# K of head 0's second half as one transfer of 128 rows, c and x as four transfers of four rows

## The chip, the cores and the metric

The kernel runs on one core of one Trainium2 chip, one launch per call. The metric is the device time of a run in microseconds (us). All times below are of the kernel with the inputs of the reference, all in bf16.

## The reference

One token passes a conditioned transformer block: an attention over a cache of 32768 positions with 8 KV heads and 32 query heads, then a small ReLU network. Cut to what matters:

```python
mod = (silu(c) @ w_mod).reshape(1, 6, 1, 512)         # c: (1, 512), w_mod: (512, 3072)
sa, ca, ga, sb, cb, gb = mod[:, 0], ..., mod[:, 5]
h = layernorm(x) * (1 + ca) + sa                      # x: (1, 1, 512)
q = (h @ wq) in 32 heads of 128                       # wq: (512, 4096)
o = softmax(q k^T / sqrt(128)) v, per head            # k, v: (8, 32768, 128), 4 query heads to each
x = x + ga * (o @ wo)                                 # wo: (4096, 512)
h = layernorm(x) * (1 + cb) + sb
x = x + gb * (relu(h @ w1) @ w2)                      # w1: (512, 1792), w2: (1792, 512)
```

K and V are 8.39 MB per head each, 134 MB together, and the weights are 15 MB. Each byte is read from HBM once and used once.

## The kernel before

The kernel is a stream of loads with the arithmetic hung beneath it. The list `stream` (lines 163 to 169) names the loads in order: K of head 0 in two halves with `w_mod` and `wq` between them, then for each head g the K of head g + 1 and the V of head g, the last heads in halves and quarters, then `wo`, `w1` and `w2` in pieces. `need(key)` (L172) issues loads from the list until the one that is asked for is out; `load` (L112) finds place and source of one; `stream_dma` (L154) issues it from SP (SyncE), so nearly all bytes go through SP's one queue. The name `UNEVEN` (L57) singles out one load, the second half of head 0's K: it goes out in three transfers (L137 to L142). The first has all 128 rows of this half without their last 512 bytes (32256 of 32768 bytes a row), the second has these last 512 bytes of rows 0 to 110, the third those of rows 111 to 127.

K and V tiles of one head (64 KB in each of 128 partitions) lie in a ring of three places. The first place holds `w_mod` and `wq`, the second K of head 0, the third K of head 1, then V of head 0 takes the first, and so on. So a load waits until the tile before it in its place has been used: V of head 0 for the last use of `wq`'s place (the product that spreads q, L409), K of head 2 for the scores of head 0 (L460). A transfer's completion is also told by one of eight semaphores in turn, and a transfer that reuses a semaphore waits for the one before on it.

`c` and `x` (512 values each) come in from ACT's queue (L182, L183) as two transfers of 8 rows of 64 values into `cx_row`. VectorE (DVE) spreads them (L248), TensorE (PE) turns them into columns (L254), and from there come silu(c) (L313 to L318) and the sums of the first layer norm (L279 to L307). Then PE multiplies silu(c) with `w_mod` (L324), the six parts of the modulation are turned back into columns (L339 to L346), the normalised h is finished (L307), q is formed with `wq` (L396) and spread (L403 to L411).

For each head, DVE transposes K in blocks of 32x32 (L332 for the first half of head 0, L441 for the rest), PE forms the scores (L460), DVE and ACT make the softmax of it (L473 to L509), and PE multiplies with V (L523). The order on PE and DVE is written out by hand (L637 to L795). In the end PE runs through `wo`, `w1` and `w2` as they land (L599, L765, L788), two DVE operations make the output (L793, L795) and SP stores it (L796).

Of the kernel before, what the change touches and what calls it, by code (L numbers as in the profile page):

```python
# [17 lines left out]
def kernel(  # L18
# [14 lines left out]
    nc = tc.nc  # L33
    P = 128
    _, _, D = A_x.shape
    _, Hkv, Sk, Dh = A_k_cache.shape
# [6 lines left out]
    TK = 64  # L43
# [10 lines left out]

    OUT0, OUT1 = 30, 34

    UNEVEN, EDGE, MOST = ("k", 0, (2, 3)), 2 * TK * Dh - D // 2, 111  # L57
    SPACE = 14
    assert Dh == 128 and REP == 4 and D == 512 and FT == W2P[-1][1] and NTILE == 4
    scale = float(Dh) ** -0.5  # L60
# [9 lines left out]
    def wo_v(i):  # L70
        g0, n = WOP[i]
        return A_wo[g0 * REP * Dh:(g0 + n) * REP * Dh, :].rearrange("(p r) d -> p r d", p=P)
# [33 lines left out]
    def piece(name, at, n):  # L106

        if name not in pieces:
            pieces[name] = ring.tile([P, NTILE * TK * Dh], BF16, tag="slot", name=name)
        return pieces[name][:, at:at + n]  # L110

    def load(key):  # L112
        kind = key[0]
        if kind == "wm":
            t = piece("wmq_sb", 0, WM).rearrange("p (kt n) -> p kt n", kt=KT)
            src = wm_v
        elif kind == "wq":
            t = piece("wmq_sb", WM, WQ).rearrange("p (kt n) -> p kt n", kt=KT)
            src = wq_v
        elif kind in "kv":  # L120
            g, steps = key[1], key[2]
            src = (kv if kind == "k" else vv)[g, :, TK * steps[0]:TK * (steps[-1] + 1), :]
            name = f"Ksb{g}" if kind == "k" else f"Vsb{g}"
            t = piece(name, TK * Dh * steps[0], TK * Dh * len(steps)).rearrange("p (j d) -> p j d", d=Dh)
        elif kind == "wo":
            g0, n = WOP[key[1]]
            t = piece("tail_sb", g0 * REP * D, n * REP * D).rearrange("p (r d) -> p r d", d=D)
            src = wo_v(key[1])
        elif kind == "w1":
            k0, k1 = W1P[key[1]]  # L130
            t = piece("tail_sb", WO + k0 * Dff, (k1 - k0) * Dff).rearrange("p (kt f) -> p kt f", f=Dff)
            src = w1_v[:, k0:k1]
        else:
            f0, f1 = W2P[key[1]]
            t = piece("tail_sb", WO + KT * Dff + f0 * D, (f1 - f0) * D).rearrange("p (f d) -> p f d", d=D)
            src = w2_v[:, f0:f1]
        if key == UNEVEN:  # L137
            row, src_row = (x.rearrange("p j d -> p (j d)") for x in (t, src))
            for rows, cols in (
                (slice(0, P), slice(0, EDGE)), (slice(0, MOST), slice(EDGE, None)), (slice(MOST, P), slice(EDGE, None)),  # L140
            ):
                stream_dma(row[rows, cols], src_row[rows, cols])  # L142
        else:
            stream_dma(t, src)
        if key[:2] == ("v", 0):
            for _ in range(SPACE):
                nc.sync.drain()
        if kind in "kv":
            for i, u in enumerate(steps):
                loaded[(kind, g, u)] = t[:, TK * i:TK * (i + 1), :]  # L150
        else:
            loaded[key] = t

    def stream_dma(dst, src):  # L154
        i = nc.sync.dma_start(out=dst, in_=src)  # L155
        tc.stamp_issue_order_token(i.ins, "sp_stream")
        if last_loop:

            tc.add_manual_dep(i.ins, last_loop[0], mybir.DependencyInfo(
                mybir.DependencyClass.NoSync, mybir.DependencyReason.DATA))  # L160
# [11 lines left out]
    def need(key):  # L172
        while key not in loaded:
            load(stream[pos[0]])
            pos[0] += 1
        return loaded[key]
# [3 lines left out]
    wm_sb = need(("wm",))  # L180
    cx_row = const.tile([16, D // 8], BF16)
    for i, row in enumerate((c[0], A_x[0, 0])):  # L182
        nc.scalar.dma_start(out=cx_row[8 * i:8 * i + 8], in_=row.rearrange("(a n) -> a n", a=8))  # L183

    ident_bf = const.tile([P, P], BF16)
    make_identity(nc, ident_bf[:])
# [10 lines left out]
        out=sel.rearrange("p (h par) (a c) -> p h par a c", h=2, a=4),  # L197
        in_=AP(ib.tensor, ib.offset, [ib.ap[0], [64, 2], [1, 2], [0, 4], [2, 32]]),
# [8 lines left out]
        out=mask16.rearrange("p (s q) -> p s q", q=REP),  # L207
        in_=AP(ident_f[:].tensor, ident_f[:].offset, [ident_f[:].ap[0], [0, 4], [1, REP], [REP, P // REP]]),
# [4 lines left out]
    for n in sorted({n * REP for _, n in WOP}):  # L213
        cmask[n] = const.tile([P, P // n], F32, name=f"cmask{n}")
        nc.vector.tensor_reduce(
            out=cmask[n][:], in_=ident_f[:].rearrange("p (c r) -> p c r", r=n), op=ALU.add, axis=AX.X,
# [3 lines left out]
            out=rsel_f[:], in_=ident_f[:].rearrange("p (c r) -> p r c", r=n), op=ALU.add, axis=AX.X,  # L220
# [6 lines left out]
        out=smask[:], in_=ident_f[0:16, 0:16].rearrange("p (s q) -> p s q", q=REP), op=ALU.add, axis=AX.X,  # L227
# [7 lines left out]
        out=place32[:], in_=ident_f[:].rearrange("p (j m) -> p m j", m=32), op=ALU.add, axis=AX.X,  # L235
# [4 lines left out]
        out=rowpick[:, OUT0:OUT1], in_=ident_f[:].rearrange("p (j m) -> p j m", m=32), op=ALU.add, axis=AX.X,  # L240
# [8 lines left out]
        out=cx_bd, in0=cx_row[:].unsqueeze(1).to_broadcast([16, 8, D // 8]),  # L249
# [80 lines left out]
    for u in range(2):  # L330
        t = need(("k", 0, u)).rearrange("p j d -> p (j d)").bitcast(F32)
# [30 lines left out]
    def four_rows(e, name):  # L362
# [16 lines left out]
        out=nca[:], in0=modT_sb[:, KT:2 * KT], scalar1=-1.0, scalar2=-1.0, op0=ALU.mult, op1=ALU.add,  # L379
# [3 lines left out]
        out=ncb[:], in0=modT_sb[:, 4 * KT:5 * KT], scalar1=-1.0, scalar2=-1.0, op0=ALU.mult, op1=ALU.add,  # L383
# [18 lines left out]
    for i in range(2):  # L402
        nc.vector.transpose(out=q_cols[:, i, :], in_=q_ps[i])  # L403
        nc.scalar.copy(
            out=qT_sb[:, 16 * i:16 * (i + 1)], in_=q_cols[:, i, :].rearrange("p (h r) -> p h r", r=32)[:, :, 0],
# [231 lines left out]
    with tc.manual_schedule(engines={mybir.EngineType.PE, mybir.EngineType.DVE}):  # L637
# [54 lines left out]
        for u in (2, 3):  # L692
# [49 lines left out]
            out=x1T[:], in0=x1T[:], scalar=1.0, in1=xT, op0=ALU.mult, op1=ALU.add, accum_out=stat2[:, 0:1],  # L742
# [31 lines left out]
        for f0, f1 in ((0, FT // 2), (FT // 2, FT)):  # L774
            nc.vector.transpose(out=hidT[:, f0:f1], in_=hid_v[:, f0:f1])
            nc.scalar.activation(
                out=AP(hb.tensor, hb.offset + 32 * f0 + 31, [hb.ap[0], [32, f1 - f0]]),
                in_=hidT[:, f0:f1, 0], func=ACT.Relu,
            )

        for part, (f0, f1) in enumerate(W2P):
            w2_sb = need(("w2", part))
            for ft in range(f0, f1):
                for i in (0, 2, 1, 3):
                    row = OUT0 + i
# [41 lines left out]
```

## Time and profile before

| what | value |
|---|---|
| time, median of 3 runs | 354.38 us (354.29 to 354.51) |
| the profiled execution | 354.42 us |
| its span, first to last instruction | 352.6 us |
| PE busy | 272.3 us, 77% of the span |
| DVE busy | 195.6 us, 55% |
| ACT busy | 18.7 us, 5% |
| transfers of SP's queue (q1), share of the 16 DMA engines | 98.5% |
| granted TensorE clock, mean | 0.926 |

How to read it: the busy shares are of one core's engines over the whole span; the share of a DMA queue is the time of all its packets over 16 engines times the span. A packet is one contiguous run of bytes, or the 4 bytes with which one DMA engine tells that its part of a transfer has landed. The rate in GB/s of a slice counts each packet where it starts, so in a slice of a few hundredths of a us a single row of K (32 or 64 KB) stands out as a large number. Times in the views count from the first instruction; between the span and the time of a run lie 354.42 - 352.6 = 1.8 us that no instruction fills.

### The profile page before, as it was taken

How to read it: one execution, taken by the hardware profiler on the slowest of the kernel's cores; microseconds unless marked ns; L12 is line 12 of the kernel's file. 1: busy time of each engine (PE TensorE's matmuls, PEld its weight loads, DVE VectorE, ACT ScalarE, POOL GpSimd, SP SyncE). 2: the span in 40 equal slices, each digit the busy share in tenths (PEclk: the TensorE clock that was granted, in tenths of full speed). 3: DMA queues.
4: the chain of work that ended last, by engine and by line, in shares of the span. 5: the costliest groups of instructions: out<-in, count | busy, mean ns of one | idle time of the engine just before them, and what ended most of it. 6: DMA issues, size and time to landing. Idle time of an engine off the chain costs nothing. (4 is left out here: it accounts for less than half of the span.)

```text
span 352.6 us, 3544 instructions
## 1 busy us (share of the span) xinstructions
PE 272.3 (77%) x1310; PEld 111.8 (32%) x1310; DVE 195.6 (55%) x167; ACT 18.7 (5%) x37; POOL 6.0 (2%) x26
## 2 busy tenths in 40 slices
PE   0054980695999679884988499976999999789994
PEld 0021330232333224331333233322444443234442
DVE  7662563983079513965099316956674293743142
ACT  1200003001000010001000100001000100011000
POOL 3000000000000000000000000000000000000000
PEclk9996895698999969998999979996999999999999
DMA  8999989999999999999999999999999999999995
GB/s 353 404 432 456 468 387 461 446 401 446 439 424 440 416 439 446 401 455 446 409 453 446 409 453 431 426 394 439 446 414 427 450 429 424 431 453 398 432 426 213
DMA packets 5222, 149.57 MB, mean 424 GB/s; under 512 B 604, under 2 KB 988, under 8 KB 1628
## 3 DMA queue, kind: packets, MB, share of 16 engines
q1 hardware_dynamic: 5180, 149.43, 98.5%
q8 instruction: 8, 0.13, 0.1%
q14 instruction: 2, 0.02, 0.0%
q10 hardware_dynamic: 32, 0.00, 0.0%
HBM read 149.42 MB, written 0.00 MB: 424 GB/s over the span
## 5 line engine op out<-in xcount | busy, mean ns | idle before, releaser
L441 DVE STREAM_TRANSPOSE Ksb<-Ksb 128x4096 f32<-128x4096 f32 (+1 forms) x34 | 131.5, 3912 | 57.6 <-DMA Ksb<-in_A_k_cache_dram 57.6
L460 PE MATMUL S_ps<-Ksb,qbd 128*128 128x512 bf16 x512 | 118.9, 385 | 19.2 <-DVE Ksb L441 18.3
L523 PE MATMUL o_ps<-Vsb,P_g 128*16 (+1 forms) x512 | 124.3, 401 | 10.9 <-ACT P_g L497 10.0
L460 PEld LDWEIGHTS <-qbd 128*128 128x128 bf16 x512 | 49.2, 97 | 84.9 <-issue 27.6
L523 PEld LDWEIGHTS o_ps<-Vsb,P_g 128*16 x320 | 30.4, 95 | 60.0 <-issue 31.8
L523 PEld LDWEIGHTS <-P_g 128*16 128x16 bf16 x192 | 16.7, 90 | 22.9 <-issue 0.4
L473 DVE TENSOR_REDUCE m_p<-S_ps 128x1 f32<-128x1024 f32 x7 | 8.6, 1223 | 21.8 <-PE S_ps L460 21.8
L502 DVE STREAM_TRANSPOSE P_g<-P_g 128x1024 bf16<-128x1024 bf16 x8 | 10.0, 1245 | 15.6 <-ACT P_g L497 15.6
L494 ACT ACTIVATE nbias<-Mb_ps 128x1 f32<-128x1 f32 x8 | 1.4, 171 | 269.5 <-PE Mb_ps L492 269.5
L324 PE MATMUL mod_ps<-wmq_sb,siluT 128*1 128x512 bf16 x24 | 3.6, 624 | 9.9 <-DMA wmq_sb<-in_w_mod_dram 9.9
L332 DVE STREAM_TRANSPOSE Ksb<-Ksb 128x4096 f32<-128x4096 f32 x2 | 8.8, 4424 | 1.7 <-DMA Ksb<-in_A_k_cache_dram 1.7
L478 PE MATMUL mT_ps<-ident_f,m_p 128*1 128x128 f32 x8 | 2.2, 270 | 8.9 <-DVE m_p L473 7.9
L497 ACT ACTIVATE P_g<-S_ps,nbias 128x1024 bf16<-128x1024 f32 x8 | 8.9, 1114 | 0.2
L560 PE MATMUL acc_ps<-mask_sb,Y 16*128 16x4 f32 x16 | 3.4, 282 | 5.1 <-DVE Y L556 5.1
L552 DVE SCALAR_TENSOR_TENSOR o_ps<-o_ps,Linv,smask 16x512 f32<-16x512 f32 x8 | 5.8, 720 | 2.8 <-PE o_ps L523 2.8
L254 PE MATMUL xc_ps<-cx_sel,wmq_sb 16*128 16x2 bf16 x4 | 0.3, 172 | 8.7 <-DVE wmq_sb L248 8.7
L590 DVE CAST o_sb<-o_ps 128x4 bf16<-128x4 f32 (+2 forms) x4 | 0.7, 167 | 11.1 <-PE o_ps L586 11.1
L415 POOL TENSOR_TENSOR qbd<-qrep_sb,rowpick 128x64 bf16<-128x64 bf16 x8 | 2.4, 299 | 228.0 <-PE S_ps L460 198.3
L509 DVE RECIPROCAL Linv<-L_ps 16x1 f32<-16x1 f32 x8 | 1.0, 126 | 8.3 <-PE L_ps L506 8.3
L556 DVE TENSOR_REDUCE Y<-o_ps 16x128 f32<-16x512 f32 x8 | 5.4, 679 | 0.3
L635 PE MATMUL spare_ps<-qbd,ident_bf 128*128 128x512 bf16 x18 | 5.4, 381 | 0.0
L396 PE MATMUL q_ps<-wmq_sb,hT 128*1 128x512 bf16 x32 | 3.6, 626 | 2.3 <-DMA wmq_sb<-in_A_wq_dram 2.3
(114 smaller groups left out, 71.6 us busy)
## 6 DMA issues: line engine op xcount, KB each, us to landing
Ksb<-in_A_k_cache_dram SPq DMA_DIRECT2D x5, 4096.0 KB, 22.9
Vsb<-in_A_v_cache_dram SPq DMA_DIRECT2D x5, 4096.0 KB, 36.5
wmq_sb<-in_A_wq_dram SPq DMA_DIRECT2D x1, 4096.0 KB, 28.1
Vsb<-in_A_v_cache_dram SPq DMA_DIRECT2D x2, 2048.0 KB, 41.1
Ksb<-in_A_k_cache_dram SPq DMA_DIRECT2D x1, 4032.0 KB, 37.2
wmq_sb<-in_w_mod_dram SPq DMA_DIRECT2D x1, 3072.0 KB, 18.9
tail_sb<-in_A_wo_dram SPq DMA_DIRECT2D x1, 2048.0 KB, 23.2
tail_sb<-in_B_w_dram SPq DMA_DIRECT2D x1, 1792.0 KB, 30.6
```

The lines of the kernel that those rows point to most:

```text
L324: nc.tensor.matmul(dst[j // 4][32 * (j % 4):32 * (j % 4) + 1, :], lhsT=src_T[:, kt:kt + 1], rhs=w[:, kt, j * 512:(j + 1) * 512], start=(kt ...
L332: nc.vector.transpose(out=t, in_=t)
L396: nc.tensor.matmul(q_ps[i][32 * a:32 * a + 1, :].rearrange("o (h e) -> o h e", e=32), lhsT=hT[:, kt:kt + 1], rhs=wq_f[:, kt, i, a], start= ...
L441: t = nc.vector.transpose(out=KTt.bitcast(F32), in_=KTt.bitcast(F32))
L460: nc.tensor.matmul(S_ps_tiles[g], lhsT=qbd[g % 2][:, hp, 4 * (7 - s):4 * (7 - s) + P], rhs=KTv[:, 16 * sl:16 * sl + 16, h, :, par], start= ...
L473: behind_loop(nc.vector.reduce_max(out=m_p[:], in_=S_g.rearrange("p g f -> p (g f)"), axis=AX.X))
L497: nc.scalar.activation(out=P_g[:], in_=S_g.rearrange("p g f -> p (g f)"), func=ACT.Exp, bias=nbias[:], scale=scale, accum_out=l_g[:],)
L502: behind_loop(nc.vector.transpose(out=P_g[:], in_=P_g[:]))
L523: nc.tensor.matmul(o_tiles[g][:], lhsT=PT, rhs=Vx, start=first, stop=False, skip_group_check=True)
L552: nc.vector.scalar_tensor_tensor(out=o, in0=o, scalar=Linv_tiles.pop(g)[:], in1=smask[:].unsqueeze(2).to_broadcast([16, 4, Dh]), op0=ALU.m ...
L556: nc.vector.tensor_reduce(out=Y[:], in_=o.rearrange("p s d -> p d s"), op=ALU.add, axis=AX.X)
L635: nc.tensor.matmul(spare[0], lhsT=ident_bf[:], rhs=qbd[0][:, :, 0:P], start=True, stop=True)
```

## The change

The name `UNEVEN` and its three transfers go: the second half of head 0's K is one transfer of 128 rows of 32768 bytes, as all other halves are. And `c` and `x` go out as four transfers of 4 rows in the place of two of 8 rows. The number of transfers stays the same, 3 + 2 before and 1 + 4 after, and so the later transfers keep their turn among the eight semaphores. The order of all other instructions on every engine is unchanged.

```diff
-    UNEVEN, EDGE, MOST = ("k", 0, (2, 3)), 2 * TK * Dh - D // 2, 111
     SPACE = 14
...
-        if key == UNEVEN:
-            row, src_row = (x.rearrange("p j d -> p (j d)") for x in (t, src))
-            for rows, cols in (
-                (slice(0, P), slice(0, EDGE)), (slice(0, MOST), slice(EDGE, None)), (slice(MOST, P), slice(EDGE, None)),
-            ):
-                stream_dma(row[rows, cols], src_row[rows, cols])
-        else:
-            stream_dma(t, src)
+        stream_dma(t, src)
...
     for i, row in enumerate((c[0], A_x[0, 0])):
-        nc.scalar.dma_start(out=cx_row[8 * i:8 * i + 8], in_=row.rearrange("(a n) -> a n", a=8))
+        for a in (0, 4):
+            nc.scalar.dma_start(
+                out=cx_row[8 * i + a:8 * i + a + 4], in_=row.rearrange("(a n) -> a n", a=8)[a:a + 4],
+            )
```

## The prediction

> **What bounds the kernel now.** I read the page's DMA part first, then the chain of work that ended last, then windows over the DMA traffic.
>
> ```profile
> span 352.6 us, 3544 instructions
> ...
> DMA packets 5222, 149.57 MB, mean 424 GB/s; under 512 B 604, under 2 KB 988, under 8 KB 1628
> ...
> q1 hardware_dynamic: 5180, 149.43, 98.5%
> q8 instruction: 8, 0.13, 0.1%
> ...
> q10 hardware_dynamic: 32, 0.00, 0.0%
> ```
>
> SP's queue keeps the 16 DMA engines busy for 98.5% of the span. The chain, in order of time, ends so:
>
> ```profile
> 338.50 11.12 DMA tail_sb<-in_B_w_dram
> ...
> 349.66 0.29 PE end_ps L788 x4
> ...
> 350.30 0.28 DVE o_bf L795
> ```
>
> The last piece of `w2` lands at 349.6 us and all that follows is under 3 us of fixed work. So the end is the end of the stream. Is the stream ever dry? The columns that count here are the last two, DMA share and GB/s:
>
> ```profile
> 12.85:21.62 8.77, 1.51 (x16) 0.51 (x17) 8.77 (x3) 0.00 (x0) 0.00 (x0) 1.00 1.01 433
> 60.00:77.00 17.00, 12.23 (x48) 5.07 (x49) 16.73 (x4) 0.00 (x0) 0.00 (x0) 0.76 1.00 432
> 200.00:300.00 100.00, 90.01 (x395) 37.65 (x396) 57.49 (x39) 4.13 (x9) 0.30 (x1) 0.93 1.00 430
> 347.80:349.60 1.80, 1.33 (x34) 1.01 (x32) 0.00 (x0) 0.00 (x0) 0.00 (x0) 1.00 0.44 158
> ```
>
> It isn't: 432 GB/s, 27.0 a DMA engine, throughout. But in the last 1.8 us the share is 0.44: some engines are done while others still carry data. The last transfer is complete when its slowest engine is, so the time is set by the engine with the most to do, and I have to ask which one that is.
>
> **The split, engine by engine.** This is the DMA traffic from 38.57 to 39.88 us in 40 slices of 33 ns, as the pieces of head 0's K go by and K of head 1 begins:
>
> ```profile
> GB/s 16 4065 2032 31 10069 31 63 4034 31 4081 47 94 2048 63 78 47 78 63 63 78 47 78 63 47 94 47 78 2048 31 47 47 47 31 47 47 47 2017 16 31 2001
> DMA packets 164, 1.11 MB, mean 851 GB/s; under 512 B 20, under 2 KB 148, under 8 KB 148
> ```
>
> A slice near 2000 is one 64 KB row of K of head 1, an engine's first (4065 is two, 10069 five). Thirteen engines reach it in slices 2 to 13, by 39.0 us. Three come in slices 28, 37 and 40, at 39.46, 39.76 and 39.86: these carry the 148 - 20 = 128 packets of 512 bytes. The one with the longest queue is 38 slices, 1.25 us, behind the first, the shortest 26 slices, 0.85. So 111 rows went to three engines at 37 each, and the 17 rows to one of the three (54 there): 0.85 / 37 is 23 ns a packet.
>
> Is one of these three the last at the end? The same view from 58.15 to 59.95 us (45 ns a slice), where V of head 0 begins, then 116.1 to 118.0 (48 ns), and what the code queue did between them (79.3 to 116):
>
> ```profile
> GB/s 1456 2913 1457 4369 0 1456 2913 0 1456 0 0 0 0 0 0 0 0 0 1456 0 0 0 0 1456 1456 0 0 1456 0 0 0 0 0 0 0 0 0 1456 0 0
> ```
> ```profile
> GB/s 1380 2760 2760 1380 1380 1380 1380 0 1380 0 0 0 0 0 0 0 0 1380 0 0 0 1380 0 1380 0 1380 0 0 0 0 0 0 0 0 0 1380 0 1380 0 0
> ```
> ```profile
> q8 instruction: 1, 0.02, 0.2%
> ```
>
> At 58 us eleven engines are together and five late, by 0.81, 1.04, 1.08, 1.22 and 1.67 us. The split explains at most 1.25, and between 40 and 58 us one code fetch of 16 KB and one smaller one went through:
>
> ```profile
> q8 instruction: 1, 0.02, 0.4%
> q14 instruction: 1, 0.01, 0.1%
> ```
>
> At 116 us, one code fetch later, ten are together and six late: one engine has gone from at most 0.38 to 1.7 us. So a code fetch costs the engine that it falls on about 1.5 us, more than the split costs any engine. The late ones stay late. Six fetches fall between 60 and 333 us. Near the end I count the engines that report the landing of one piece of `wo` (the packets under 512 bytes) in three stretches, 333.85 to 334.35, to 335.20, and to 335.70:
>
> ```profile
> q8 instruction: 6, 0.10, 0.1%
> ```
> ```profile
> DMA packets 21, 0.20 MB, mean 410 GB/s; under 512 B 5, under 2 KB 5, under 8 KB 5
> ```
> ```profile
> DMA packets 35, 0.34 MB, mean 395 GB/s; under 512 B 4, under 2 KB 4, under 8 KB 4
> ```
> ```profile
> DMA packets 30, 0.19 MB, mean 377 GB/s; under 512 B 7, under 2 KB 7, under 8 KB 7
> ```
>
> 5, 4 and 7, where 58 us had 11, 4 and 1. Six fetches moved six engines from the first group to the last; the middle group, in which the split's three stand (0.81 to 1.22), hasn't changed. So the end is set by a group of **seven engines that each took a code fetch and none of the split**.
>
> **The change, part by part.** *K as one transfer.* Each engine now carries its 8 rows whole: 8 x 512 = 4096 bytes more at 27.0 GB/s, **+0.15 us**. The three lose their small packets and gain 0.15: about -0.7, -0.7 and -1.1 us. As they were 0.5 us or more ahead of the last group, that buys nothing, while the last group comes 0.15 us later, and with it the end. Every landing before it moves by the same 0.15, so the work that waits for landings moves along.
>
> *What SP issues.* Two transfers fewer. Their issue stands in the second row here:
>
> ```profile
> 1.35 0.28 ACTq L183 DMA_DIRECT2D cx_row<-in_A_x_dram  x1
> ...
> 2.12 20.71 SPq L155 DMA_DIRECT2D Ksb<-in_A_k_cache_dram  x4
> ...
> 7.99 0.68 DVE L248 TENSOR_TENSOR wmq_sb<-cx_row,pick 16x512 bf16<-16x512 bf16 x1 [1.50 <-DMA cx_row<-in_A_x_dram]
> ...
> 10.98 0.16 DVE L318 TENSOR_TENSOR siluT<-xc,sig 128x4 bf16<-128x4 f32 x1
> ...
> 12.85 8.77 DVE L332 STREAM_TRANSPOSE Ksb<-Ksb 128x4096 f32<-128x4096 f32 x2 [1.71 <-DMA Ksb<-in_A_k_cache_dram]
> 20.11 3.57 PE L324 MATMUL mod_ps<-wmq_sb,siluT 128*1 128x512 bf16 x24 [9.91 <-DMA wmq_sb<-in_w_mod_dram]
> ...
> 24.34 0.69 DVE L340 COPY wmq_sb<-mod_ps 128x512 f32<-128x512 f32 x1 [2.67 <-ACT wmq_sb L339]
> ...
> 27.28 0.22 DVE L307 SCALAR_TENSOR_TENSOR hT<-cen_ln,rstd_ln,modT_sb 128x4 bf16<-128x4 f32 x1
> ...
> 29.79 3.58 PE L396 MATMUL q_ps<-wmq_sb,hT 128*1 128x512 bf16 x32 [2.31 <-DMA wmq_sb<-in_A_wq_dram]
> ...
> 35.36 0.35 SPq L155 DMA_DIRECT2D Vsb<-in_A_v_cache_dram  x1
> ```
>
> SP sat until 22.8 us on four issues, and may now be free earlier. It gains nothing: its next act, V of head 0 at 35.36, waits for q, and the data of K of head 1 keeps the engines busy to 58.2 us (row above). The cover is 22.8 us.
>
> *c and x in four transfers.* ACT issues two more, some 0.28 each. The price is in the queue. x was issued at 1.35 and used at 7.99. Its packets, in the windows 5.9 to 6.5 and 7.2 to 7.7:
>
> ```profile
> q10 hardware_dynamic: 8, 0.00, 1.1%
> ```
> ```profile
> q10 hardware_dynamic: 8, 0.00, 0.9%
> ```
>
> Eight rows on eight engines, and 1.2 us later their eight reports: an engine puts one K packet (32 KB, 1.21 us) between two small ones. The first part of c still goes ahead of K as c does now; three transfers then take two turns each in place of one transfer's two, 4 x 1.21 = 4.85 us more. L248 would start at 12.8 and L318 end at 16.0. The other bound is nothing, if all go in x's turns; I take the slow one. The transposes of L332 then start 3.1 us late and end at 24.8, L340 moves from 24.34 to 24.9, L307 ends at 28.1, and L396 waits for `wq` until 29.79 as before. L324 isn't touched (16.0 against 20.11). So **0**, with 1.7 us of cover left, and behind that V's 22.8. On the engines themselves a pair of small packets is 1.1% x 16 x 0.6 / 8 + 0.9% x 16 x 0.5 / 8 = 0.02 us. An engine gets two pairs more or less, at most 0.045 us either way. Which engines these are no row tells. The Trainium skill (DMA: Bandwidth & Descriptors, "Why a DMA increments its semaphore by 16 and not by 1") says that such a transfer takes the lowest-numbered ones, those of the split here: by that the last group could only lose packets, and the sum would be 0.11 to 0.15.
>
> **Sum**: +0.15 us (0.11 to 0.20). The profiled 354.42 becomes 354.57; it lies 0.04 above the median, so against the median of 354.38 I predict 354.53. That is 0.04%. A measurement of this kernel can tell about 0.2%, 0.7 us, from no change, so it should read as the same.
>
> **The rivals.**
>
> *One shared limit.* If the rate were one of all engines together, who carries which bytes wouldn't matter. The change would save only what small packets cost more than their bytes, 128 x (23 - 19) ns / 16 = 0.03 us: 354.35. The Trainium skill (DMA: Bandwidth & Descriptors, "Where 436 GB/s comes from") says that the HBM side, at about 358 GB/s, binds such loads; by it the change would be worth nothing. The row of 432 GB/s is above that figure. And where fewer engines are at work (0.44) the rate falls with them to 158: those left don't speed up. 12%.
>
> *A second fetch on one engine* (slower). The engine of a code fetch isn't named in the program. The eight so far seem to fall on different ones. If after the change a fetch falls on an engine of the last group, that one is 1.5 us further behind: 354.53 + 1.45 = 356.0. It decides if it comes before the engine's last bytes, at 349 us. Against: the fetches are PE's code for the most part, which is unchanged, and three more engines are free to take one. 7%.
>
> *The split's engines end last after all* (faster). Were all seven of the last group wrongly assigned and the longest queue of the split the last, it would lose 1.1 us: 353.3. The counts 5, 4, 7 and the 1.67 us that no split gives speak against it. 4%.
>
> *The cover in front is too short* (slower). Should each of the three small transfers wait as long as x did, 6 us, L248 comes at 20 and V's issue some 8 us late, still 15 us ahead of need. It costs from 58.2 us on; 1%, in the slow case below.
>
> **How the numbers follow.** Forecast 74%, 354.3 to 354.8; shared limit 12%; second fetch and short cover 8%; split's engines last 4%; something else 2%. The first two, 86%, hold a range of 354.2 to 354.9 with the scatter of the runs (0.1 either way). Both are within 0.2%. So faster 0.05, same 0.86, slower 0.09.
>
> **What would show it.** In the profile after: 5222 - 132 = 5090 packets (128 small ones and their 4 reports), q10 still 32. In the window after 38.6 us all sixteen engines begin K of head 1 within half a us. Near the end the middle group has one engine, not four, the last still seven, and the last `w2` lands 0.15 us later. L248 starts near 12.8 and L396 still at 29.8 to 30.0. It is wrong if L396 or V's issue moves by several us and the share falls below 1.00 near 58 us, or if the last group has an engine 3 us behind the first.

## The result and the profile after

The changed kernel takes 355.27 us (median of 16 runs, 354.89 to 355.48) against 354.21 before (median of 15 runs, 354.07 to 354.56): a ratio of 1.0028, with an interval of 1.0021 to 1.0034. A sixteenth run of before took 370.82 us, in a slower state that a few executions show, and such runs are left out of all figures here. The change makes the kernel 1.0 us slower. The direction of the sum was right, its size was not: 0.15 us were forecast, and 355.27 lies above the range of 354.2 to 354.9. The profiled execution is at 355.27 with a span of 353.2 us, so the span grew by 0.6 and what lies outside it from 1.8 to 2.05.

First the page of the changed kernel, to see that the change does what it says:

```profile
span 353.2 us, 3545 instructions
...
DMA packets 5090, 149.57 MB, mean 423 GB/s; under 512 B 600, under 2 KB 856, under 8 KB 1496
...
q10 hardware_dynamic: 32, 0.00, 0.0%
```

5090 packets and 32 on ACT's queue, as worked out. The traffic from 38.6 to 39.9 us, again in slices of 33 ns, shows the split gone: all sixteen engines begin K of head 1 in the first 19 slices, none comes behind.

```profile
GB/s 2017 0 0 2017 0 4033 6050 2017 0 2017 0 2017 2017 0 2017 4033 2016 0 2017 0 0 0 0 0 0 0 0 0 0 0 0 0 0 0 0 0 0 0 0 0
```

Near the end the engines that report one piece of `wo` are counted in three stretches as before (333.90 to 334.40, to 335.25, to 335.80):

```profile
DMA packets 25, 0.20 MB, mean 393 GB/s; under 512 B 8, under 2 KB 8, under 8 KB 8
```
```profile
DMA packets 35, 0.35 MB, mean 414 GB/s; under 512 B 1, under 2 KB 1, under 8 KB 1
```
```profile
DMA packets 31, 0.20 MB, mean 358 GB/s; under 512 B 7, under 2 KB 7, under 8 KB 7
```

8, 1 and 7, where before had 5, 4 and 7: the three engines of the split are now with the first, and the last group is the seven that it was. So where is the time? The chain of the changed kernel, in order of time:

```profile
338.55 11.11 DMA tail_sb<-in_B_w_dram
...
349.71 0.29 PE end_ps L783 x4
...
350.34 0.28 DVE o_bf L790
```

The last `w2` lands 0.05 us later than before and the output is made 0.04 us later (350.34 against 350.30), in this pair of executions. Of 0.6 us in the span over 0.5 come **after the arithmetic is over**, in the closing instructions, of which the prediction had said only that they are fixed. There SyncE waits on the semaphores of all loads, last on the landing of the output, and then tells the other engines (the line is that of the end of the program, L822 before and L817 after). The recorded instructions of SyncE on that line, before, in the stretches 351.0 to 351.5, to 351.7, to 351.86 and to 352.0; the last columns are the first and last start in us:

```profile
L822 SPq EVENT_SEMAPHORE  x3: 28/28/28, 351.0 to 351.2; - x3
```
```profile
L822 SPq EVENT_SEMAPHORE  x1: 28/28/28, 351.6 to 351.6; - x1
```
```profile
L822 SPq EVENT_SEMAPHORE  x1: 28/28/28, 351.8 to 351.8; - x1
```
```profile
L822 SPq DRAIN  x2: 7/7/7, 351.9 to 351.9; - x2
```

And after, 351.0 to 351.5, to 351.9, to 352.6:

```profile
L817 SPq EVENT_SEMAPHORE  x5: 28/28/28, 351.1 to 351.3; - x5
```
```profile
L817 SPq EVENT_SEMAPHORE  x1: 28/28/28, 351.9 to 351.9; - x1
```
```profile
L817 SPq DRAIN  x2: 7/66/124, 352.3 to 352.5; - x2
```

Both have a gap of over 0.4 us in which SyncE does nothing. Before, it lies between 351.2 and 351.6, and the wait for the output's landing is answered only at 351.8: the gap costs nothing. After, the five waits run through by 351.3, the output has landed at 351.9, and then comes the gap, to 352.3, with a first drain of 124 in place of 7 ns. In both programs the instruction behind the gap is the 80th that the trace records of SyncE: two transfers fewer have moved the gap two instructions on, from under the landing to behind it.

### The profile page after: what moved, and what is told of

It is laid out like the page before. It is cut to its first block, busy times and chain, and to the rows that moved or that the text cites. A ratio compares the mean times of both kernels' runs of the same rounds, so it can differ in the third digit from the quotient of the medians.

```text
span 353.2 us, 3545 instructions
## 1 busy us (share of the span) xinstructions
PE 275.1 (78%) x1310; PEld 112.6 (32%) x1310; DVE 195.5 (55%) x167; ACT 18.7 (5%) x37; POOL 6.0 (2%) x26
## 2 busy tenths in 40 slices
DMA packets 5090, 149.57 MB, mean 423 GB/s; under 512 B 600, under 2 KB 856, under 8 KB 1496
## 5 line engine op out<-in xcount | busy, mean ns | idle before, releaser
L518 PE MATMUL o_ps<-Vsb,P_g 128*16 (+1 forms) x512 | 126.1, 407 | 10.7 <-ACT P_g L492 10.0
L476 DVE TENSOR_REDUCE Mrow<-mT_ps 1x4 f32<-1x128 f32 x8 | 2.2, 274 | 5.6 <-PE mT_ps L473 5.6
```

Of the source, the lines that this page charges most:

```text
L518: nc.tensor.matmul(o_tiles[g][:], lhsT=PT, rhs=Vx, start=first, stop=False, skip_group_check=True)
```

## The experiments

Theory A: the stop of 0.42 us belongs to a place in SyncE's program; the two transfers that went made it visible. Rivals: B, the balance of the DMA engines is worth the whole; C, c and x in four transfers cost it in the front. Each run of a chip gives its time and its span, so I can split a difference in two: that of the span, and that of the rest (time less span). All means are over 9 to 11 runs of each experiment, 16 of the changed kernel, and 19 to 34 of before on the same chip; the error of a mean span is about 0.05.

| kernel | time, median | before, median | span less before's | rest |
|---|---|---|---|---|
| changed kernel | 355.27 | 354.21 | +0.8 (353.16) | 2.06 |
| e1_pad16 | 354.54 | 354.14 | +0.22 | 2.04 |
| e4_pad15 | 354.50 | 354.14 | +0.21 | 2.05 |
| e6_pad22 | 354.52 | 354.19 | +0.11 | 2.05 |
| e9_pad13 | 355.08 | 354.23 | +0.67 | 2.07 |
| e2_split_pad12 | 354.79 | 354.14 | +0.59 | 1.81 |
| e3_thirds | 354.40 | 354.14 | +0.24 | 1.80 |
| e5_act2 | 354.46 | 354.19 | +0.01 | 2.01 |
| e5_act8 | 354.42 | 354.19 | +0.21 | 1.82 |
| e7_edge1024 | 355.05 | 354.19 | +0.77 | 1.80 |
| e8_split_pad22 | 354.36 | 354.23 | +0.05 | 1.80 |

The kernel before has a rest of 1.80 and a mean span of 352.38 to 352.45 on these chips; the runs of before that stood beside the changed kernel list no spans, so its +0.8 is against 352.4.

**e1_pad16.** The changed kernel, its program for SyncE as long as before:

```diff
-    SPACE = 14
+    SPACE = 16
```

> The changed kernel with 16 in place of 14 empty instructions (drains) behind the load of V of head 0, so that SyncE's program has as many instructions as before. Theory A (SyncE's program stops for 0.42 us at a fixed place, its 80th recorded instruction; two transfers fewer move that place from under the output's landing to behind it): most of the 1.0 us comes back, 354.3 to 354.5, and the profile shows the stop of 0.42 us ahead of the wait for the output, not behind it. Rival B (the balance of the DMA engines is worth it all): 355.3 as without the two. Rival C (c and x in four transfers, landing 4.9 us later): 355.3.

354.54: 0.73 us come back. The closing of this kernel, 350.8 to 351.3, to 351.6, to 351.7, to 351.9:

```profile
L817 SPq EVENT_SEMAPHORE  x4: 28/28/28, 350.9 to 351.1; - x4
```
```profile
L817 SPq EVENT_SEMAPHORE  x1: 28/28/28, 351.5 to 351.5; - x1
```
```profile
L817 SPq EVENT_SEMAPHORE  x1: 28/28/28, 351.6 to 351.6; - x1
```
```profile
L817 SPq DRAIN  x2: 7/7/7, 351.7 to 351.8; - x2
```

The gap is back ahead of the wait. B and C fall as causes of the whole. The ratio to before, 1.0013 (1.0004 to 1.0022), isn't 1: a second and a third cause remain.

**e2_split_pad12.** The kernel before, two instructions shorter for SyncE and nothing else:

```diff
-    SPACE = 14
+    SPACE = 12
```

> The kernel before, split and all, with 12 in place of 14 drains: SyncE's program is two instructions shorter, as in the changed kernel, and no byte of the loads is moved. Theory A: 0.5 to 0.9 us slower than before, 354.8 to 355.1, with the stop of 0.42 us behind the wait for the output. Rivals B and C: no change, 354.25.

354.79, ratio 1.0017 (1.0008 to 1.0026). The stop alone, with the split in place, costs 0.59 us of span and nothing in the rest. SyncE's closing, 350.8 to 351.3, to 351.8 and to 352.4, is that of the changed kernel:

```profile
L822 SPq EVENT_SEMAPHORE  x5: 27/28/28, 350.9 to 351.1; - x5
```
```profile
L822 SPq EVENT_SEMAPHORE  x1: 28/28/28, 351.7 to 351.7; - x1
```
```profile
L822 SPq DRAIN  x2: 7/65/123, 352.2 to 352.3; - x2
```

**e3_thirds.** The kernel before with three transfers of all rows:

```diff
-    UNEVEN, EDGE, MOST = ("k", 0, (2, 3)), 2 * TK * Dh - D // 2, 111
+    UNEVEN, THIRDS = ("k", 0, (2, 3)), (0, 5440, 10912, 2 * TK * Dh)
...
+            for c0, c1 in zip(THIRDS, THIRDS[1:]):
+                stream_dma(row[:, c0:c1], src_row[:, c0:c1])
```

> The kernel before with the second half of head 0's K in three transfers of all 128 rows, a third of each row in each (10880, 10944 and 10944 bytes): the DMA engines carry equal bytes as in the changed kernel, but SyncE's program, the turn of the semaphores and c and x are as before. Theory A: the balance alone, 0.15 us for 4096 bytes more on each of the thirteen engines: 354.3 to 354.5. Rival B: 355.3. Rival C: 354.25.

354.40, ratio 1.0006 (0.9997 to 1.0015): by itself not to be told from 1. But the whole K adds to the span in all four kernels that have it without a visible stop, +0.24, +0.22, +0.21 and +0.11, 0.20 on average. Three of them have c and x in four transfers as well, and they add no more than this one: C has no part in the span that these runs could tell.

**e4_pad15, e6_pad22 and e9_pad13** move the stop further: `SPACE = 15`, `22` and `13` in the changed kernel.

> The changed kernel with 15 drains, one more. Theory A: the stop falls just ahead of the wait for the output's landing, which comes 0.5 us after the instruction before it, so it is covered: 354.3 to 354.6, as with 16. If the stop isn't tied to a place in SyncE's program, or is of some other length, 355.3 as with 14. Rivals B and C: 355.3.

> The changed kernel with 22 drains: by theory A the stop of SyncE's program now falls on the wait ahead of the output's transfer, at 340 us, where SyncE has ten us to spare. Time as with 15 and 16 drains, 354.4 to 354.7, and no stop of 0.4 us between the last wait and the closing drain. If the stop belongs to the closing instructions themselves or comes when the output lands, 355.2.

> The changed kernel with 13 drains, one fewer. Theory A: the stop falls one instruction further behind the wait for the output, on the closing drain that tells the other engines; still not covered, 355.0 to 355.3. If only the one drain of the changed kernel stops, 354.6.

354.50, 354.52 and 355.08: with 15, 16 and 22 the stop is covered, with 13 and 14 it isn't. With 13 it has moved from the first closing drain to the second, which now starts 0.4 us after the first and is the one that takes 125 ns (352.3 to 352.9):

```profile
L817 SPq DRAIN  x2: 7/66/125, 352.3 to 352.8; - x2
```

With 22 there is none left between the last wait and the closing drains (351.5 to 351.6, then to 352.0):

```profile
L817 SPq EVENT_SEMAPHORE  x1: 28/28/28, 351.6 to 351.6; - x1
```
```profile
L817 SPq DRAIN  x3: 7/7/7, 351.6 to 351.9; - x3
```

In that kernel a packet of 8 KB on the code queue q14, which before ran at 352.3 and after at 353.2, runs between 341 and 344 us:

```profile
q14 instruction: 1, 0.01, 0.6%
```

So the packet moves with the stop, and that suggests the loading of a block of SyncE's code. But the packet starts only after the stop is over (352.3 against 351.6 before, 353.2 against 352.3 after), so it isn't this packet that SyncE waited for. The trace doesn't name what SyncE waits for: shown is that the stop belongs to a place in the program, and its nature stays open. The Trainium skill (Runtime: NRT & Kernel Launch, "Instruction fetch mechanics") says that the sequencer fetches its code in blocks by its own DMA queue and that the crossing of a boundary is mostly hidden. If the stop is such a crossing, these runs agree with "mostly": hidden under any longer wait, and 0.57 us of the time where none is left.

**e5_act2 and e5_act8** ask for the rest. All kernels with c and x in four transfers had 2.04 to 2.07 us there, those with two 1.80. In the kernel before, behind the loads of c and x:

```diff
+    for _ in range(2):        # 8 in e5_act8
+        nc.scalar.drain()
```

> The kernel before with two drains in ACT's program behind the loads of c and x, in place of two more loads: ACT's program is as long as in the changed kernel, and every transfer is as before. All four kernels with c and x in four transfers had 2.03 to 2.06 us between span and time, the others 1.80 to 1.83. Theory A2 (the length of ACT's program costs 0.24 us behind the span): 354.3 to 354.5, 2.0 us or more outside the span, the span as before (352.4). Rival D (it is the two more transfers, or where c and x land): no change, 354.15, 1.8 us outside.

> The same with eight drains. If the 0.24 us come with a place in the program that is passed (a further block of code to be loaded), they come once: 354.3 to 354.5. If each instruction costs something at the end, 0.12 us each, 1.0 us: 355.1. Rival D: 354.15.

354.46 and 354.42, ratios 1.0008 (0.9999 to 1.0017) and 1.0007 (0.9998 to 1.0016): by the time alone not to be told from 1. The rest, with an error of at most 0.03, and the span show more. Two empty instructions on ACT do what the two additional transfers do: the rest goes to 2.01 (2.04 without one execution of the eleven, which has 1.75), the span stays. With eight it costs as much, once and not fourfold, but within the span (+0.21, rest 1.82). There the trace shows it. These are ACT's closing drains of the kernel before and of e5_act8 (351 to 354 us):

```profile
L822 ACTq DRAIN  x1: 14/14/14, 352.2 to 352.2; - x1
```
```profile
L824 ACTq DRAIN  x1: 138/138/138, 352.4 to 352.4; - x1
```

In e5_act8 this drain is the 64th of ACT's 65 recorded instructions. It starts 0.38 us after the end of the one ahead of it, where before it is 0.08, and takes 138 in place of 14 ns, much as at SyncE's stop. So it too is a place in a program, ACT's this time, and not the transfers. With two more instructions ACT has 59 recorded, and a 64th would lie behind the end of the span, where the rest has grown; that this is the same stop is argued, as the trace ends there. In e5_act2 and the changed kernel a further 8 KB of code is fetched after 353.3 us (first and second row), of which the kernel before has none there:

```profile
q14 instruction: 1, 0.01, 0.8%
```
```profile
q14 instruction: 1, 0.01, 0.9%
```

Rival D is out. Which engine waits for what behind the span, and why the kernel before doesn't pay there, the trace doesn't record.

**e7_edge1024** tests the account of each DMA engine by overdoing the split:

```diff
-    UNEVEN, EDGE, MOST = ("k", 0, (2, 3)), 2 * TK * Dh - D // 2, 111
+    UNEVEN, EDGE, MOST = ("k", 0, (2, 3)), 2 * TK * Dh - D, 111
```

> The kernel before with the last 1024 in place of 512 bytes of each row split into 111 and 17 rows. By the account of each DMA engine (theory A): thirteen engines are relieved of 0.3 us, the one with 54 packets carries 54 x about 0.04 = 2.3 us more and comes in behind those with a code fetch (1.7): 0.2 to 0.5 us slower than before, 354.4 to 354.65. If what counts is the relief of the thirteen alone: 0.15 us faster, 354.0. If all engines share one limit: no change, 354.15.

355.05, ratio 1.0022 (1.0013 to 1.0032), +0.77 us of span: slower, as the account has it, though thirteen engines carry less; both rivals in this expectation fall. The size was too small. The traffic from 38.4 to 41.4 us (slices of 75 ns, K of head 1 begins at about 874 a row):

```profile
GB/s 874 4369 874 1748 1802 68 1816 68 82 68 68 82 68 82 55 82 68 82 68 68 68 68 41 55 68 41 915 27 888 27 14 14 27 14 14 27 14 27 888 874
```

The three come in slices 27, 29 and 39; the last slice is already a second row of another engine. Their small packets begin in slice 5 (1802 is two rows and four packets), 0.3 us behind the first row. From there it is 1.65 us for 37 packets and 2.55 for 54, so 45 to 47 ns a packet of 1024 bytes and not the 40 that I took. The last `w2` then lands 0.6 us later, as the chain shows:

```profile
350.30 0.29 PE end_ps L788 x4
```

**e8_split_pad22** looks for a version that beats both: the kernel before with `SPACE = 22`.

> The kernel before with 22 in place of 14 drains, which puts SyncE's stop at 340 us, ten us ahead of the output. Theory A: in the kernel before the stop ends at 351.66 and the output lands at 351.78, so it is covered already and nothing is to be had: 354.1 to 354.25. If a part of the stop still shows there, up to 0.4 us faster: 353.8, and this would be the fastest version.

354.36, ratio 1.0001 (0.9991 to 1.0011): 0.1 above the expected range by its median, level with before by the ratio. Nothing more is to be had there, and no kernel here is faster than the one before.

## Why the prediction was right and wrong

The sum of the causes is 0.57 (the stop, e2 and the changed kernel against e1: 0.59 and 0.56) + 0.20 (whole K) + 0.24 (ACT's program; e5_act2 alone gives 0.21) = 1.0 us, which is what was measured. Only the second term was in the forecast.

- *The stream is never dry and its slowest engine sets the end*: right. The three groups came out as 8, 1 and 7, and e7 shows that the engine with the most to do decides.
- *+0.15 us for 4096 bytes more on each engine*: right in sign, and 0.20 with about 0.03 of error, at the upper bound of 0.11 to 0.20. In the pair of profiles it is only 0.05, but single executions scatter too much for that to tell: the spans of one kernel spread by 0.1 to 0.2 (standard deviation). Whether a small further cost stands behind 0.20 is open.
- *c and x land 4.85 us later and cost nothing in the front*: right. These rows of the changed kernel answer to L248, the transposes and the product with `wq`:

```profile
12.89 0.68 DVE L243 TENSOR_TENSOR wmq_sb<-cx_row,pick 16x512 bf16<-16x512 bf16 x1 [6.41 <-DMA cx_row<-in_A_x_dram]
```
```profile
29.86 3.58 PE L391 MATMUL q_ps<-wmq_sb,hT 128*1 128x512 bf16 x32 [1.61 <-DMA wmq_sb<-in_A_wq_dram]
```

  L248 (now L243) was forecast for 12.8, and of the cover of 1.7 us ahead of `wq` 1.6 is left. The aside that the last group could only lose small packets doesn't follow, though: four rows go on four engines, the split has three, and the fourth could be one of the last group.
- *What SP issues: two transfers fewer, gains nothing*: **this step failed.** It asked what SyncE does next and stopped at the load of V of head 0. What the two instructions do to the rest of SyncE's program wasn't asked: everything behind them stands two places earlier, and a stop at a fixed place fell out of its cover. Forecast was 0, measured 0.57 us.
- *ACT issues two more, some 0.28 us each*: failed in the same way. Its program is two instructions longer, and that cost 0.24 us behind the span, where 0 was forecast.
- *All that follows is under 3 us of fixed work*: wrong, and the root of both. The closing had been read as a constant; SyncE's part of it has a stop of 0.42 us, and the rows of before show that only the wait for the output hides it.
- The rivals: none of them came. Neither the second fetch nor a shared limit is seen. The chance of 0.09 for slower held nothing but the loads and the front, and what came was in neither.

## What to carry to other kernels

To take out or add an instruction is to move all that stand behind it on that engine: look at the end of each engine's program for stops that a wait covers now, and count how many instructions of room there are. In a kernel that is bound by its loads, compare versions with the same number of instructions on each engine (empty ones will do), or a few tenths of a us from the closing are taken for the effect of the change. And bytes are worth moving only from the DMA engine that ends last, with the small packets that this takes priced on the one that receives them.

## What the hardware showed

- SyncE stops for some 0.42 us at its 80th recorded instruction in every one of these programs where no longer wait covers it, and where that instruction is a drain, it takes 124 in place of 7 ns; exposed, the two cost 0.57 us.
- A longer program on ACT, by two instructions, costs 0.24 us after the last recorded instruction; longer by eight, 0.2 before it, where ACT stops for 0.38 us at its 64th recorded instruction, a drain that takes 138 in place of 14 ns.
- A packet of 1024 bytes took 45 to 47 ns where one of 512 took 23: twice the bytes, twice the time.
